# A new order of steps on five engines and in the load queue, in a fused linear-attention and dense-Mish kernel

## The chip, the cores and the metric

The kernel runs on one core of one Trainium2 chip. The metric is device time in microseconds of one launch. Three runs of the kernel before gave 151.34, 151.38 and 151.34 us; their median is 151.34. A profile of one execution lies beside them. Its span, from the first instruction to the last, is 148.7 us.

The core has five engines, each with a queue of its own that runs strictly in program order: TensorE (PE, with its weight loads as PEld), VectorE (DVE), ScalarE (ACT), GpSimd (POOL) and SyncE (SP), which here only issues DMAs. Engines wait for each other through semaphores.

## The reference

x has 2048 tokens of 448 columns. It is normalised per token, and two branches work on the result: a linear attention with 16 heads of 28 columns, whose feature map is softmax(p) beside softmax(-p), and a dense layer of 1792 columns with a Mish activation. The three are summed. Cut to what matters:

```python
xn = _layernorm(x)                                       # (1, 2048, 448)
q, k, v = heads of xn @ wqkv                             # 16 heads of 28
pq, pk = q @ w_phi, k @ w_phi                            # per head
phi_q = concat(softmax(pq), softmax(-pq))                # 56 features
phi_k = concat(softmax(pk), softmax(-pk))
kv, z = phi_k^T v, sum over tokens of phi_k
o = (phi_q kv) / (phi_q z + 1e-6)
h = xn @ w1 + b1                                         # 1792 columns
act = h * tanh(log(1 + exp(h)))                          # Mish
out = x + o @ wo + act @ w2
```

## The kernel before

**Tiles.** The tokens lie in 16 tiles t of 128; a pair of tiles is a unit u, 0 to 7. All of x stays in SBUF (x_all). The normalised x of a unit (xn, four buffers in turn) is transposed into xnT, seven blocks of 128 columns. w_phi is folded into the key and query weights at the head of the program: the key weights are transposed by TensorE (L556), multiplied by a block-diagonal Wbd (L580), and evacuated from PSUM into Wpk; the query weights come transposed by DMA and give Wpq.

**Order.** Nothing in the program decides at run time. The string ORDER lists 341 steps. `run_order` calls them one after another; each step appends its instructions to the queues of its engines and takes PSUM banks (four pairs of banks, the one used longest ago first). Waits follow from what each instruction reads and writes. So a step's place decides its place in the queue of every engine that it uses, and also which PSUM bank it waits for.

**Steps, by name** (a last letter a, d, p, m or s says the engine: ACT, DVE, POOL, DMA, SP; b says ACT and DVE):

- `lx..`, `lkm`, `lkt`, `lvm`, `lqT`, `lp`, `l1`, `l2`, `lo`: loads on SP (x; key, value and query weights; w_phi as Wraw; W1, W2, Wo). `lx0` to `lx3` carry one unit each, `lx4` and `lx6` two.
- `st`, `rs`, `xn`, `xt`: mean and variance of a unit (`st2b` and `st3b` leave one tile of the unit to ACT, L453 to L458), 1/std, normalisation (L497 on DVE, L492 on POOL), transposition (L505 on PE with an evacuation, or L517 by DMA).
- `z12`: twelve matmuls on zeros (L364) ahead of all others. `wtk`, `wmk`, `wmq`: the folding of the weights.
- `v`, `k`, `q` with parts A, B, H: value, key and query projections of a unit (L423). A and B are six matmuls of 64 rows each, H two, 448 columns wide. Two matmuls on different halves of the array run at the same time. After a unit's last part its result is evacuated: value to v_all (L510 on ACT or L512 on DVE), key and query as two exponentials on ACT (L618, L680).
- `kn`: normalisation of one sign of the keys of a unit: sum (L626) and reciprocal (L628) on DVE, product (L630) on POOL. Both signs of all eight units: 16 of them.
- `kv`: phi_k^T v of a unit, 32 small matmuls (L649), summed over all units in one bank. `ep`: the epsilon column (L353, L356, DVE). `kvz`: the sum goes to KVT (L660, DVE) and by DMA transposition to KVZ (L666).
- `e`: DMA transposition of a tile's query features to EqT (L688). `f`: one of 28 blocks of the dense layer (L423, 512 columns, parts A, B, H as above), with its Mish on ACT (L699). `nd`: numerator and denominator of a tile (L722) and seven DVE instructions. `ot`: DMA transposition of a unit's o (L757). `wo`, `g`: the output products (L845, L828). `sto`: stores.

The steps that the change touches at the head are these: `ln_stats` reads x and is the first thing that DVE and ACT do; `ln_pair` writes xn; `xT` transposes it; `w_tr` and `w_mm` fold the weights. The last of the folding's evacuations is what the first key matmul waits for.

Of the kernel before, what the change touches and what calls it, by code (L numbers as in the profile page):

```python
# [38 lines left out]
class Program:  # L39
# [46 lines left out]
    def dma(self, eng, fn, r=(), w=(), tag=""):  # L86
        return self.op(eng, fn, r, w, dma=True, tag=tag)
# [57 lines left out]


ORDER = """
pv table lx2s lba zero pm st2b lx3s lkms lps st3b lkts z12 pi b1 rs2p pw rs3a xn2d bd lx1s wtk0b lvms lx4s xn3d xt2b
wtk1b wmk0b lqT2 xt3a v2Ha wmk1a v2Ba lqT0 st1 v3Ha lqT1 lqT3 rs1a v3Aa v2Aa st4 rs4p pk v3Ba k3H lx0s k3A qd xn1d
wmq0d wmq1a k2H k3B lx6s pp k2A st5 q3A xn4d k2B q3B rs5p q2A xt1m l1ts q3H k1A q2H xn5p xt4m st0 v1Ad k1H st6 xt5m e7  # L150
rs0p q2B st7 xn0d v1Bd k1B v1Hd rs7p rs6p k4A k4H q1B k4B xn6d q1H q1A v4Ad k5H xn7d v4Hd k5A v4Bd v5Ad kn1.0 xt0m k5B
v5Bd k0B xt6m v5Hd xt7m v0Ba kn2.1 kn2.0 k0H k0A e3 k6H k6A kn0.0 e2 v6Ba l1ms k6B v0Ha kn0.1 v0Aa v6Aa v6Ha k7H k7A
q4B e6 k7B v7Aa v7Ha kn7.0 q4H q4A q6A q6H v7Ba e9 q6B kn6.0 f0.2B kn5.1 f0.0A f1.2A f0.2A f0.0H f1.2H kn6.1 e5 f1.3B
f0.2H f0.0B e12 f1.2B f1.3A kn4.1 f0.3B kn5.0 f1.3H e13 f0.3H f0.1B e4 f0.3A f0.1H f0.1A q7H q0A kn3.1 q0H kn4.0 q5B
e8 q0B q7B kv5 kn7.1 e0 kv0 kv2 q7A q5A f0.13A q5H f0.13B kv7 kv4 e10 kv6 f0.13H f0.6H f0.6A kn3.0 f0.10A f0.6B kn1.1
f0.10B kv3 kv1 ep f0.10H f1.7H f1.7A e11 f1.9A kvz f1.7B f0.12B f1.5B f0.12A f1.5H f0.5H f1.9H f0.12H l2s f1.9B f1.5A
f0.5A f1.1A nd3 f1.1B f0.5B e15 f1.0A f1.1H f1.13B f1.0H f1.13H f1.0B nd2 los f1.13A ot1m f1.8B f0.9H f1.8A f1.8H nd0
f0.11B f0.9A f0.11A f0.11H f0.7A f0.7H f0.8B nd6 e14 f0.8H f0.9B f0.7B e1 f0.8A f1.12H f1.12A f1.10A nd7 f1.10B f1.4H
f1.10H f1.12B ot3m f1.4A nd1 f1.6B f1.4B f0.4H f1.6A ot0m f0.4A wo1H f1.6H f0.4B nd4 wo1A wo3A wo1B wo3H nd5 ot2m g1
g3 g2 f1.11A f1.11H nd11 wo0B f1.11B wo3B wo0A nd13 wo0H nd10 g6 ot5m g0 g7 g11 nd12 wo2A wo5A sto1 ot6m wo5H wo2B  # L160
nd15 nd9 g10 sto0 g5 nd14 ot7m wo2H wo5B nd8 g4 g9 g14 g13 g12 g8 sto3 ot4m wo4H wo4A wo6B wo7B sto2 wo6H wo6A sto5
wo4B sto4 wo7H wob wo7A g15 stt14 sto6 stt15
"""


# [5 lines left out]
def _kernel(es, nc, A_x, A_wqkv, A_w_phi, A_wo, B_w1, B_b1, B_w2, out):  # L171
    def sb(name, shape, dtype):
        return es.enter_context(nc.sbuf_tensor(name, shape, dtype))
# [20 lines left out]
    xnT = sb("xnT", [P, NU, 7, P], BF16)  # L194
# [58 lines left out]
    def bank16(b):  # L253
        return PS.bitcast(BF16)[:, 2 * b * TCW:2 * (b + 1) * TCW]
# [7 lines left out]
    def pb(b):  # L262
        return ("ps", b)
# [238 lines left out]
    def transpose7(e, b, src, cut=7):  # L502
        for c in range(7):
            to = bank16(b)[:, c * P:(c + 1) * P] if c < cut else bank16(b + 1)[:, (c - cut) * P:(c - cut + 1) * P]
            ins = e.transpose(to, src[:, c * P:(c + 1) * P], ident[:])  # L505
        return ins

    def evac(eng, dst, src, r, w, tag):
        if eng == "ACT":
            op("ACT", lambda e: e.activation(dst(), src(), ACT.Copy), r=r, w=w, tag=tag)  # L510
        else:
            op("DVE", lambda e: e.tensor_copy(dst(), src()), r=r, w=w, tag=tag)  # L512

    def xT(u, eng):
        i = u % NXN
        if eng == "DMA":
            dma("SP", lambda e: e.dma_start_transpose(xnT[:, u, :, :], xn[i][:, :]),  # L517
                r=[("xn", i, 0, 0), ("xn", i, 1, 0), ("xn", i, 1, 1)], w=[("xnT", u), ("xnU", u)], tag=f"xTm{u}")
            return
        if eng == "both":  # L520
            b = take2(False)
            pe(lambda e: transpose7(e, b, xn[i], 3), [("xn", i, 0, 0), ("xn", i, 1, 0), ("xn", i, 1, 1), ("ident",)],
               [pb(b), pb(b + 1)], f"xT{u}")
            evac("ACT", lambda: xnT[:, u, 0:3, :].rearrange("p c n -> p (c n)"), lambda: bank16(b)[:, 0:3 * P], [pb(b)],
                 [("xnT", u)], f"xTe{u}")
# [453 lines left out]
```

## Time and profile before

| | us |
|---|---|
| median of three runs | 151.34 |
| span of the profiled execution | 148.7 |
| of it PE busy | 144.3 |
| DVE, ACT, POOL busy | 102.4, 74.5, 38.8 |
| end of PE's last matmuls of L828 at full width | 145.67 |

For the profiled execution no time but its span is given; the median of the runs lies 2.64 us above it.

How to read it: the page gives each engine's busy time and its share of the span, then the chain of work that ended last, by engine and line. A line of the code can carry several kinds of work: L423 serves the projections of v, k and q and the dense layer, told apart by the tiles' names (Wkv, Wpk, Wpq, W) and widths. A timeline row says when a group of instructions started, how long it lasted, engine, line, output and inputs, and in brackets for how long its engine had been idle and what ended that. A row of waits says which engine and line waited for which, the sum, how often, and the longest. The key tiles' exponentials lie in rows of actT, so L630 is written actT<-actT,rSk.

### The profile page before, as it was taken

The numbers are of one execution on the slowest core, as the hardware profiler recorded it, in microseconds if no ns is written. First come the engines' busy times: TensorE is split into PE (matmuls) and PEld (weight loads), VectorE is DVE, ScalarE is ACT, GpSimd is POOL, SyncE is SP. The second block draws the span as 40 slices with busy tenths as digits, with TensorE's granted clock in tenths as the row PEclk, the third lists the DMA queues.
The fourth block names the chain that finished last, engine by engine and source line by source line (L and its number), as shares of the span: only waits on it lengthen the run. The fifth ranks groups of instructions, "written<-read, shape, count | busy, mean of one in ns | idle before, by whom it ended". The sixth has DMA issues, their size and how long they took to land.

```text
span 148.7 us, 3867 instructions
## 1 busy us (share of the span) xinstructions
PE 144.3 (97%) x1669; PEld 74.4 (50%) x1669; DVE 102.4 (69%) x229; ACT 74.5 (50%) x91; POOL 38.8 (26%) x53
## 2 busy tenths in 40 slices
PE   6999999999999999999999999999999999999993
PEld 2375555555544554444544445545555555555562
DVE  0599898996999940407697879539983999930072
ACT  3987999879999999657757762002000000000000
POOL 4423475079999993000000000000000000000000
PEclk9999999999999999999999999999999999999999
DMA  4998678799499159399856053120013040542005
GB/s 133 240 270 232 138 143 158 128 169 334 102 194 191 30 49 132 69 223 283 225 120 121 0 66 62 27 39 0 7 21 102 20 108 0 123 100 85 4 0 185
DMA packets 39964, 17.23 MB, mean 116 GB/s; under 512 B 33932, under 2 KB 39180, under 8 KB 39948
## 3 DMA queue, kind: packets, MB, share of 16 engines
q1 hardware_dynamic: 39776, 16.89, 53.4%
q8 instruction: 13, 0.21, 0.6%
q10 hardware_dynamic: 172, 0.10, 0.2%
q14 instruction: 3, 0.02, 0.0%
HBM read 7.02 MB, written 1.84 MB: 60 GB/s over the span
## 4 chain that ended last, share of the span: by engine, by line
PE 96%; DVE 1%; POOL 0%; issue 0%; POOLq 0%
PE PS L423 50%; PE PS L828 29%; PE PS L845 7%; PE PS L364 4%; PE PS L722 3%; PE PS L649 2%; PE PS L580 1%; DVE xn L497 1%; PE PS L505 1%; DVE x_all L793 0%; POOL v_all L339 0%; PE PS L556 0%; DVE x_all L814 0%; DVE b1T L512 0%; PE PS L693 0%
## 5 line engine op out<-in xcount | busy, mean ns | idle before, releaser
L423 PE MATMUL PS<-xnT,W 64*128 64x512 bf16 x392 | 44.8, 377 | 0.0
L828 PE MATMUL PS<-W,actT 128*128 128x448 bf16 (+1 forms) x224 | 42.9, 351 | 0.0
L699 ACT ACTIVATE actT<-PS,b1T 128x1024 bf16<-128x1024 f32 x28 | 29.8, 1112 | 22.1 <-PE PS L423 22.1
L828 PEld LDWEIGHTS PS<-W,actT 128*128 128x128 bf16 x224 | 21.5, 98 | 19.8 <-issue 0.3
L423 PEld LDWEIGHTS PS<-xnT,W 64*128 64x128 bf16 x392 | 18.0, 94 | 21.9 <-PE PS L423 1.9
L630 POOL TENSOR_TENSOR actT<-actT,rSk 128x896 bf16<-128x896 bf16 x16 | 26.6, 1699 | 5.1 <-DVE rSk L628 5.1
L793 DVE TENSOR_TENSOR x_all<-PS,x_all 128x448 bf16<-128x448 f32 (+1 forms) x16 | 9.2, 614 | 15.1 <-PE PS L845 10.5
L626 DVE TENSOR_REDUCE Sk<-actT 128x32 f32<-128x896 bf16 x16 | 16.6, 1037 | 1.1 <-ACT actT L618 1.1
L618 ACT ACTIVATE actT<-PS 128x896 bf16<-128x896 f32 x16 | 13.7, 920 | 1.8 <-PE PS L423 1.7
L423 PE MATMUL PS<-Wpk,xnT 64*128 64x448 bf16 x112 | 13.2, 349 | 0.0
L423 PE MATMUL PS<-Wkv,xnT 64*128 64x448 bf16 x112 | 12.9, 349 | 0.0
L423 PE MATMUL PS<-Wpq,xnT 64*128 64x448 bf16 x112 | 12.6, 349 | 0.0
L738 DVE COPY Sq<-PS 128x16 f32<-128x16 f32 x32 | 4.0, 167 | 12.0 <-PE PS L722 12.0
L462 DVE BATCH_NORM_STATS2 stats<-x_all 128x6 f32<-128x448 bf16 x14 | 8.4, 601 | 3.5 <-DMA x_all<-in_A_x_dram 3.5
L746 DVE TENSOR_TENSOR v_all<-v_all 128x464 f32<-128x464 f32 x16 | 10.3, 642 | 0.6
L742 DVE TENSOR_TENSOR v_all<-PS,Sq 128x464 f32<-128x464 f32 x16 | 10.3, 641 | 0.5
L749 DVE TENSOR_TENSOR xn<-v_all,rden 128x448 bf16<-128x448 f32 x16 | 10.0, 626 | 0.6
L744 DVE TENSOR_TENSOR v_all<-PS,Sq 128x464 f32<-128x464 f32 x16 | 10.1, 630 | 0.0
L680 ACT ACTIVATE actT<-PS 128x896 bf16<-128x896 f32 x10 | 8.6, 930 | 0.1
L423 PEld LDWEIGHTS PS<-Wpq,xnT 64*128 64x128 bf16 x112 | 5.4, 94 | 5.0 <-ACT actT L680 0.2
L423 PEld LDWEIGHTS PS<-Wkv,xnT 64*128 64x128 bf16 x112 | 5.4, 94 | 5.0 <-ACT actT L618 0.2
L423 PEld LDWEIGHTS PS<-Wpk,xnT 64*128 64x128 bf16 x112 | 5.4, 94 | 5.1 <-issue 0.2
(83 smaller groups left out, 119.3 us busy)
## 6 DMA issues: line engine op xcount, KB each, us to landing
W<-in_B_w_dram SPq DMA_DIRECT2D x1, 1568.0 KB, 9.3
out_dram<-x_all SPq DMA_DIRECT2D x7, 224.0 KB, 2.2
W<-in_B_w_dram SPq DMA_DIRECT2D x1, 1344.0 KB, 6.5
x_all<-in_A_x_dram SPq DMA_DIRECT2D x4, 224.0 KB, 3.0
x_all<-in_A_x_dram SPq DMA_DIRECT2D x2, 448.0 KB, 4.7
Wkv<-in_A_wqkv_dram SPq DMA_DIRECT2D x2, 336.0 KB, 5.1
Wo<-in_A_wo_dram SPq DMA_DIRECT2D x2, 336.0 KB, 5.9
W<-in_B_w_dram SPq DMA_DIRECT2D x2, 224.0 KB, 3.6
```

The lines of the kernel that those rows point to most:

```text
L423: ins = e.matmul(o, lhs(c, k), rhs(c, k), start=first and n == at[par][0], stop=last and n == at[par][-1])
L618: op("ACT", lambda e, s=s: e.activation(E_of(u)[:, s, :, :], two(b, D), ACT.Exp, scale=1.0 if s == 0 else -1.0), r=[pb(b), pb(b + 1)], w=[ ...
L626: op("DVE", lambda e: e.tensor_reduce(Sk[u][:, s, :], Eh(), AX.X, ALU.add), r=[("E", u, s)], w=[("Sk", u, s)], tag=f"Sk{u}.{s}")
L630: op("POOL", lambda e: e.tensor_tensor(Eh(), Eh(), ap_on(rSk[u][:, s, 0:1], [[1, 2 * H], [0, DH]]), ALU.mult), r=[("E", u, s), ("rSk", u, ...
L699: op("ACT", lambda e: e.activation(actT[:, fc, q * 1024:(q + 1) * 1024], bank(b, 2), ACT.Mish, bias=b1T[:, fc:fc + 1]), r=[("b1T",), pb(b) ...
L742: op("DVE", lambda e: e.tensor_tensor(tv(t1[i]), num(0), sx(1), ALU.mult), r=[pb(b), pb(b + 1), ("Sq", i, 1)], w=[("t1", i)], tag=f"ta{t}")
L744: op("DVE", lambda e: e.tensor_tensor(tv(t2), num(1), sx(0), ALU.mult), r=[pb(b), pb(b + 1), ("Sq", i, 0)], w=[("t2",)], tag=f"tb{t}")
L746: op("DVE", lambda e: e.tensor_tensor(t1[i], t1[i], t2, ALU.add), r=[("t1", i), ("t2",)], w=[("t1", i)], tag=f"tc{t}")
L749: op("DVE", lambda e: e.tensor_tensor(o_sb[(t // 2) % 2][:, t % 2, :].rearrange("p (h d) -> p h d", d=DH), t1[i][:, :, 0:DH], ap_on(rden[i ...
L793: op("DVE", lambda e: e.tensor_tensor(x_all[:, t, 0:n], bank(b)[:, 0:n], x_all[:, t, 0:n], ALU.add), r=[pb(b), ("x", t)], w=[("out", t)], ...
L828: ins = e.matmul(bank(b)[:, 0:width(t)], actT[:, fc, tok(t)], W2[:, fc, 0:width(t)], start=first and fc == 0, stop=last and fc == FC - 1)
L845: ins = e.matmul(bank(b)[:, 0:w], oT_of(u)[lo:hi, cc * P:(cc + 1) * P], Wo[lo:hi, cc, 0:w], start=first and n == at[par][0], stop=last and ...
```

## The change

The table ORDER is replaced, and one label in `xT` changes, which names an instruction and has no effect on it. The steps are the same ones, but for the engine letter of some: the evacuations of `xt2`, `wtk0` and `wtk1` go from two engines to one, unit 1 is transposed by TensorE in place of unit 3, unit 3 is normalised by POOL in place of DVE, the 1/std of units 2 and 4 is made by ACT and that of unit 3 by POOL, the two `wmq` change their engines, and the evacuations of the value tiles are shared out anew (units 1, 2, 3, 4 on ACT and 0, 5, 6, 7 on DVE; before, 0, 2, 3, 6, 7 and 1, 4, 5). One line of the table, and the label:

```diff
-pv table lx2s lba zero pm st2b lx3s lkms lps st3b lkts z12 pi b1 rs2p pw rs3a xn2d bd lx1s wtk0b lvms lx4s xn3d xt2b
+lx2s lx1s zero lkms lps pi lx3s table lkts lba pm st2b rs2a st1 xn2d rs1a pw xn1d z12 st3b wtk0d lvms xt2a b1 lx4s
...
-                 [("xnT", u)], f"xTe{u}")
+                 [("xnT", u)], f"xTh{u}")
```

What stands in the queues now is seen best in rows of the two programs, engine by engine, in program order.

**ScalarE at the head.** Rows are line, operation, output and inputs, size. L453 to L458 are the statistics of one tile (the tile of unit 2 stands above these rows in both), L476 and L478 make 1/std of a unit, L510 are evacuations of PSUM. Before:

```order
L453 ACTIVATE junk,mv<-x_all 128x448
L456 ACTIVATE rmean<-mv 128x1
L458 ACTIVATE junk,mv<-x_all,rmean 128x448
L476 ACTIVATE lnv<-mv,eps_col 128x2
L478 ACTIVATE rstd<-lnv 128x2
L510 ACTIVATE Eq<-PS 112x512
L510 ACTIVATE xnT<-PS 128x384
L510 ACTIVATE Eq<-PS 112x512
L510 ACTIVATE Wpk<-PS 128x448
L510 ACTIVATE xnT<-PS 128x896
L510 ACTIVATE Wpk<-PS 128x896
L476 ACTIVATE lnv<-mv,eps_col 128x2
```

and now:

```order
L476 ACTIVATE lnv<-mv,eps_col 128x2
L478 ACTIVATE rstd<-lnv 128x2
L476 ACTIVATE lnv<-mv,eps_col 128x2
L478 ACTIVATE rstd<-lnv 128x2
L453 ACTIVATE junk,mv<-x_all 128x448
L456 ACTIVATE rmean<-mv 128x1
L458 ACTIVATE junk,mv<-x_all,rmean 128x448
L510 ACTIVATE xnT<-PS 128x896 x2
L510 ACTIVATE Wpk<-PS 128x448
L510 ACTIVATE Wpk<-PS 128x896
L476 ACTIVATE lnv<-mv,eps_col 128x2
```

The statistics of unit 3's tile have moved behind the 1/std of units 2 and 1, and the four evacuations behind them are now two whole units of xnT and the two of Wpk. In SP's queue the x of unit 3 moves at the same time from second place to fifth, behind x of units 2 and 1, the key weights and Wraw.

**VectorE at the end of the key normalisation.** The number in Sk and rSk is the unit. L512 are value tiles, L353 and L356 the epsilon column, L660 the first thing done with the sum of kv. Before:

```order
L626 TENSOR_REDUCE Sk3<-actT 128x32
L628 RECIPROCAL rSk3<-Sk3 128x32
L626 TENSOR_REDUCE Sk1<-actT 128x32
L628 RECIPROCAL rSk1<-Sk1 128x32
L353 TENSOR_REDUCE epsT<-ident 128x1 x2
L356 SCALAR_TENSOR_TENSOR epsT<-epsT 128x1
L660 TENSOR_SCALAR KVT<-PS,epsT 30x8x28 x4
```

and now:

```order
L512 CAST v_all<-PS 128x32x28 x2
L626 TENSOR_REDUCE Sk0<-actT 128x32
L628 RECIPROCAL rSk0<-Sk0 128x32
L353 TENSOR_REDUCE epsT<-ident 128x1 x2
L356 SCALAR_TENSOR_TENSOR epsT<-epsT 128x1
L626 TENSOR_REDUCE Sk6<-actT 128x32
L628 RECIPROCAL rSk6<-Sk6 128x32
L626 TENSOR_REDUCE Sk6<-actT 128x32
L628 RECIPROCAL rSk6<-Sk6 128x32
L626 TENSOR_REDUCE Sk7<-actT 128x32
L628 RECIPROCAL rSk7<-Sk7 128x32
L626 TENSOR_REDUCE Sk5<-actT 128x32
```

The epsilon column has moved ahead of the last four normalisations (units 6, 6, 7 and 5), and two value tiles (units 6 and 0) stand just ahead of it. POOL's products follow the same order: its last four are those of units 6, 6, 7 and 5.

**TensorE around kv.** L649 is kv, L722 is nd, L423 with W is the dense layer and with Wpq the query projection. Before:

```order
L423 MATMUL PS<-Wpq,xnT 128x448 x28
L649 MATMUL PS<-actT,v_all 30x56 x96
L423 MATMUL PS<-Wpq,xnT 128x448 x12
L423 MATMUL PS<-xnT,W 128x512 x6
L423 MATMUL PS<-Wpq,xnT 128x448 x2
L423 MATMUL PS<-xnT,W 128x512 x6
L649 MATMUL PS<-actT,v_all 30x56 x96
L423 MATMUL PS<-xnT,W 128x512 x28
L649 MATMUL PS<-actT,v_all 30x56 x64
L423 MATMUL PS<-xnT,W 128x512 x72
L722 MATMUL PS<-KVZ,EqT 128x60 x16
```

and now:

```order
L423 MATMUL PS<-Wpq,xnT 128x448 x6
L423 MATMUL PS<-xnT,W 128x512 x2
L649 MATMUL PS<-actT,v_all 30x56 x256
L423 MATMUL PS<-xnT,W 128x512 x46
L722 MATMUL PS<-KVZ,EqT 128x60 x16
```

The three groups of kv have become one of 256 matmuls, in the order of units 3, 6, 4, 2, 7, 0, 5, 1, and 46 matmuls of the dense layer, in place of 72, stand between it and the first use of KVZ.

Three more moves matter for queues. On DVE the normalisation of units 6 and 7 (six instructions of L497) now comes after the first sum and reciprocal of a key unit (unit 2), whose product is the first of its kind on POOL; before, all of L497 came ahead of all of L626. On SP the main part of W1 now stands ahead of the transpositions of units 0, 6 and 7 (L517); before, behind them. And where nd had been mixed with g through the last third of the program, all dense blocks and thirteen of the sixteen nd now come ahead of the first g, so that g runs in three stretches of four, four and eight tiles.

More of the change, by code (lines that the diff above doesn't have):

```diff
@@ L147 @@
 ORDER = """
-pv table lx2s lba zero pm st2b lx3s lkms lps st3b lkts z12 pi b1 rs2p pw rs3a xn2d bd lx1s wtk0b lvms lx4s xn3d xt2b
[L149 to L162, printed above, removed]
+lx2s lx1s zero lkms lps pi lx3s table lkts lba pm st2b rs2a st1 xn2d rs1a pw xn1d z12 st3b wtk0d lvms xt2a b1 lx4s
@@ new lines @@
+bd xt1a lx0s rs3p wtk1d wmk0b wmk1a v2Ha xn3p lqT3 lqT0 st4 v1Ad rs4a lqT2 lqT1 v1Bd st5 k2H v2Ba xn4d lx6s v1Ha pp
+v2Aa xt3m qd k2A rs5p k2B xn5p st0 xt4m k1H wmq1d wmq0a k1A k1B st6 k3H l1ts xt5m st7 rs0p xn0d l1ms k3A xt0m q1H
+rs6p k3B k4H rs7p k4A k4B v4Hd kn2.1 q1B xn6d q1A q3H xn7d v4Ba v4Aa kn4.1 v5Ha q3B q3A v5Ad q2H v5Bd k5H kn2.0 q2A
+kn1.0 xt6m kn1.1 pv q2B k5A xt7m k5B v3Bd k7H k7B v3Ha k7A kn4.0 v7Ha v3Aa q4H v7Bd e7 v7Ad k0A e3 k0B kn3.0 k0H q6H
+q4A e2 e6 q4B e4 e5 kn7.1 q6B k6B v0Aa k6H q6A kn5.1 v0Ha kn0.1 v6Ba v6Aa k6A kn3.1 v6Hd e9 q5A v0Bd kn0.0 ep q5H
@@ new lines @@
+q5B e8 q7H kn6.1 q7B f1.3H q7A f1.3B kn6.0 f1.3A f0.0A f0.0H f1.1H f1.1B f1.1A f0.0B los f1.0H e14 f1.0A e13 f1.0B
+q0B kn7.0 q0H f1.2H e12 f1.2B q0A kn5.0 f0.8H kv3 pk e10 kv6 kv4 kv2 kv7 kv0 e15 kv5 kv1 f0.8B e1 f0.8A f0.2H kvz
+f0.2A e11 e0 f1.2A f0.2B f1.6H wob f0.5B f0.5A nd2 f1.6B f0.5H nd3 f1.6A f1.5H f1.5B f1.5A f0.10H f0.10A f0.10B
+f0.7H nd1 ot1m f0.11H f0.7A f0.7B f0.13H f0.13B f0.13A f0.3B nd6 f0.3H f0.11B f0.11A f0.6A nd7 f0.3A f0.6H f1.11H
+f0.6B f1.11B nd0 f0.4H f1.11A ot3m f0.4B ot0m f0.9H f0.9A f0.4A f0.12H nd4 f0.12B f0.12A f0.9B f1.7A nd10 l2s f1.13H
@@ L163 @@
+f1.13B f1.7B f1.7H f1.10H f1.10B f1.13A f1.10A f1.9B nd5 f1.9H f0.1H f0.1A f1.9A ot2m nd13 f1.4H f1.4B f0.1B f1.4A
+f1.8H f1.8A wo1A nd12 wo1H f1.12B f1.12A f1.12H f1.8B wo1B wo0A wo0B nd11 ot6m ot5m wo0H nd15 g0 g1 g3 g2 nd9 wo6A
+wo6H wo2H nd8 wo2B wo6B wo2A nd14 ot4m ot7m sto0 g12 g4 g13 g5 wo4H wo7B wo5H wo4A sto1 wo3H wo5B wo7H wo3B wo7A
+wo4B wo5A wo3A g10 g11 g14 stt14 g6 sto5 g9 g7 sto3 g8 sto2 sto6 g15 sto4 stt15
 """
```

## The prediction

> **What bounds the kernel now.** First the page: busy times (part 1) and the chain that ended last (part 4).
>
> ```profile
> PE 144.3 (97%) x1669; PEld 74.4 (50%) x1669; DVE 102.4 (69%) x229; ACT 74.5 (50%) x91; POOL 38.8 (26%) x53
> ...
> PE 96%; DVE 1%; POOL 0%; issue 0%; POOLq 0%
> ```
>
> TensorE is busy for 144.3 of 148.7 us and the chain lies on it for 96%. A busy share can hide waits, so next the waits of TensorE, and the chain in order of time (start, duration, what).
>
> ```profile
> PE PS L364 <- POOL mask L327: 1.4, 1, 1.4
> PE PS L505 <- DVE xn L497: 0.3, 1, 0.3
> PE PS L556 <- DMA Wkv<-in_A_wqkv_dram: 0.2, 1, 0.2
> ```
>
> ```profile
> 1.39 5.30 PE PS L364 x12
> ...
> 10.72 3.32 PE PS L423 x34
> ...
> 51.18 0.88 PE PS L649 x96
> ...
> 54.84 0.88 PE PS L649 x96
> ...
> 58.84 0.61 PE PS L649 x64
> 59.45 7.90 PE PS L423 x72
> ...
> 90.76 0.22 PE PS L722 x16
> ...
> 113.91 0.33 PE PS L722 x16
> ...
> 143.25 2.42 PE PS L828 x14
> 145.67 0.02 issue
> 145.69 0.56 DVE x_all L793
> ```
>
> All waits of TensorE end before 9 us. From 10.72 it runs at one pace to 145.67: 34 matmuls of 448 columns in 3.32 are 0.098 us each, 72 of 512 columns in 7.90 are 0.110. So a new order can win only at the head, at the switches between matmul shapes, and behind 145.67, where the last bank's addition and store stay as they were. It can lose wherever TensorE is made to wait. The matmuls are the same, so I add up delays of TensorE against this trace.
>
> **A. The head: +0.65 us.** Unit u is a pair of token tiles. The new load queue sends x of pair 1 second and x of pair 3 fifth. ScalarE still makes half of pair 3's statistics (L453 to L458), and these now stand in its queue ahead of both evacuations of the transposed x (xnT) and of both of Wpk; the first key matmul needs the last of them. Timeline of the head, and two rows of the DMA issues (KB each, us to landing):
>
> ```profile
> 2.20 0.49 SPq L293 DMA_DIRECT2D Wraw<-in_A_w_phi_dram  x1
> ...
> 2.72 1.20 SPq L278 DMA_DIRECT2D Wkv<-in_A_wqkv_dram  x2
> ...
> 3.54 0.58 ACT L453 ACTIVATE junk<-x_all 128x448 bf16<-128x448 bf16 x1 [1.46 <-DMA x_all<-in_A_x_dram]
> ...
> 5.14 0.56 ACT L453 ACTIVATE junk<-x_all 128x448 bf16<-128x448 bf16 x1
> ...
> 9.67 0.54 ACT L510 ACTIVATE Wpk<-PS 128x448 bf16<-128x448 f32 x1
> ...
> 9.86 0.36 PE L423 MATMUL PS<-Wkv,xnT 64*128 64x448 bf16 x2
> 10.09 0.92 ACT L510 ACTIVATE xnT<-PS 128x896 bf16<-128x896 bf16 x1
> ...
> 10.65 2.63 PE L423 MATMUL PS<-Wkv,xnT 64*128 64x448 bf16 x26
> ...
> 10.89 0.93 ACT L510 ACTIVATE Wpk<-PS 128x896 bf16<-128x896 f32 x1
> ```
>
> ```profile
> Wkv<-in_A_wqkv_dram SPq DMA_DIRECT2D x2, 112.0 KB, 5.0
> ...
> Wraw<-in_A_w_phi_dram SPq DMA_DIRECT2D x1, 24.5 KB, 5.0
> ```
>
> When does x of pair 3 land? It now stands right behind Wraw, which lands at 2.20 + 5.0 = 7.2. The 224 KB that stood there, two halves issued from 2.72 to 3.92, landed by about 8.4. The same bytes for x, so 7.2 to 8.4; I take 7.85, the middle. Then ScalarE needs 1.60 for the statistics (3.54 to 5.14), 0.80 for each xnT (10.09 to 10.89), 0.42 for the small Wpk (9.67 to 10.09) and 0.93 for the large one: 4.55, and about 0.05 to wake TensorE. Key matmuls start at 12.45. Ahead of them stand 14 value matmuls; before, two went at 9.86 and the next twelve from 10.65, so the 14th was done at 10.65 + 12 x 0.098 = 11.8. The delay is 12.45 - 11.8 = 0.65. Bounds: 0 (7.2) to 1.2 (8.4). The first warm-up starts some 0.4 earlier, but the matmul behind it still waits for Wkv, so that buys nothing.
>
> **B. Two waits inside the projections: +0.85 us together.** DVE and POOL rows of the key normalisation, DVE first:
>
> ```profile
> 49.08 1.03 DVE L626 TENSOR_REDUCE Sk<-actT 128x32 f32<-128x896 bf16 x1
> 50.14 0.35 DVE L628 RECIPROCAL rSk<-Sk 128x32 f32<-128x32 f32 x1
> 50.41 1.03 DVE L626 TENSOR_REDUCE Sk<-actT 128x32 f32<-128x896 bf16 x1
> ...
> 51.94 1.64 DVE L356 SCALAR_TENSOR_TENSOR epsT<-epsT 128x1 f32<-128x1 f32 x1
> ```
>
> ```profile
> 46.90 9.98 POOL L630 TENSOR_TENSOR actT<-actT,rSk 128x896 bf16<-128x896 bf16 x6
> ```
>
> ```profile
> 50.22 3.35 POOL L630 TENSOR_TENSOR actT<-actT,rSk 128x896 bf16<-128x896 bf16 x2
> ...
> L512 DVE CAST v_all<-PS 128x896 bf16<-128x896 f32 x2 | 2.2, 1090 | 0.1
> ```
>
> One half of a pair's normalisation costs DVE 1.33 (49.08 to 50.41) and POOL 1.66 (9.98 / 6). Before, the eight kv steps (L649) stood in three groups spread from 51 to 59 us, so POOL's multiplications ended beside them. Now all eight stand in one run, and the seventh, kv5, needs POOL's last product. Worse, the epsilon steps (L353, L356) have moved from the end of DVE's normalisations to a place ahead of the last four. The one-column L356 took 1.64 us: it started at 51.94 and ended at 53.58, and POOL's multiplication ended at 50.22 + 3.35 = 53.57. It waited for POOL. In the new order it starts just after rSk of pair 0, which also releases a POOL multiplication, so it will wait a whole one, and DVE's next normalisation, for which POOL waits, is late by that.
>
> The chain from the last value pass of pair 0: 0.2 to wake DVE, 1.0 for its evacuation (1.09 less overlap), 1.39 for the sum and reciprocal, 1.70 behind POOL, 1.41 for the next sum and reciprocal, 4 x 1.66 on POOL: 12.35 us. TensorE's own work between the same two points: 36 matmuls at 0.098, 66 at 0.110, six kv steps of 0.27 (0.88 - 0.61) and a switch: 12.5. No slack is left, and DVE reaches that evacuation with a full queue: from its evacuation of pair 5 it has 3 x 1.0 + 9 x 1.33 = 15.0 us, plus a wait of about 0.4 for pair 7, against 158 matmuls, 14.9 to 15.5 us. I expect kv5 to wait 0.3 to 0.6.
>
> The other place is the key matmul of pair 7, which waits for the DMA transposition of its x. That is issued when DVE has normalised pair 7, and these six instructions (L497) now stand beside POOL's first multiplication.
>
> ```profile
> L497 DVE TENSOR_SCALAR xn<-x_all,mv,rstd x6: 286/374/622, 6.9 to 8.8; 128x448 bf16<-128x448 bf16 x2, 128x64 bf16<-128x64 bf16 x2, 128x384 bf16<-128x384 bf16 x2
> ```
>
> ```profile
> W<-in_B_w_dram SPq DMA_DIRECT2D x1, 1344.0 KB, 6.5
> ...
> xnT<-xn SPq DMA_TRANSPOSE x6, 3.1
> ```
>
> The 622 ns one lay beside a POOL product, so at least 0.25 was lost there (622 - 374). Carried along the new order with the durations above, the transposition lands within 0.1 us of its use if POOL lets DVE by, and up to 0.9 late if DVE waits a whole POOL instruction (1.66, less the slack). The 1344 KB of W1 now also go ahead of the last three transpositions. Both waits overlap, since a wait at pair 7 gives POOL time: together 0.3 to 1.8, and I take 0.85, nearer to the rows (0.25 and 0.3 to 0.6 measured or worked out) than to the worst.
>
> [...]
>
> **C. The wait for KVZ: +0.25.** From the end of kv to the landing of its transposition:
>
> ```profile
> 59.59 1.83 DVE L660 TENSOR_SCALAR KVT<-PS,epsT 30x224 bf16<-30x224 f32 x4 [6.01 <-PE PS L649]
> ```
>
> ```profile
> 61.46 1.23 SPq L666 DMA_TRANSPOSE KVZ<-KVT  x1
> ...
> DMA to landing us min/median/max: 3.2/3.2/3.2
> ```
>
> That is 64.66 - 59.45 = 5.2 us. Before, 72 matmuls (7.9 us) covered it; now 46 stand between, 5.05 us, so with the wake-up a wait of 0.1 to 0.4.
>
> **D. Fewer switches: -0.75.** Where matmuls of 128 rows meet those of 64, or of 56 (L722), the step is longer: 0.33 against 0.22. Such meetings fall from nine to five: -0.45. The kv steps in one run take 0.61 + 6 x 0.27 = 2.23, not 2.37, and two entries into them go, at 0.11 each: -0.35 in all. I take -0.75; 0 to -0.9.
>
> **Sum.** 0.65 + 0.85 + 0.25 - 0.75 = +1.0 us. Of the profiled execution only the span is told: 148.7 becomes 149.7. The median lies 2.64 above the span (151.34 - 148.7), which I add unchanged: **152.3 us**. Behind kv I find no other wait: the weights W2 are issued far ahead of the first L828, and each bank taken for L722 is free again one or two units later.
>
> **Rivals.** *No blocking (0.15):* L356 gets in between two POOL instructions. The chain to kv5 is 1.5 shorter, B is zero, and A + C + D = +0.15: 151.5. Against it: the place of L356 right behind what releases POOL. *Faster (0.15):* TensorE's own path decides everywhere. Its place is the load of pair 3's x: landing at 7.2, just behind Wraw, makes A zero; with B at zero too, only C and D are left, -0.5: 150.85. It decides once x lands before about 7.5 and L356 isn't blocked. For it speaks that nothing else in the new order costs TensorE time. *Much slower (0.15):* DVE waits for POOL at pair 7 in full and x lands at 8.4: A 1.2, B 1.6, C 0.3, D -0.75, so +2.35: 153.7. [...] The forecast keeps 0.55.
>
> **The numbers.** The forecast's own range is 151.8 to 153.0. Eight in ten needs most of the no-blocking case and of the much slower one: 151.0 to 153.6. Within 0.2% (0.3 us), about what a measurement of this kernel can tell from no change, lies the no-blocking case: 0.15. Faster takes 0.15, slower 0.70.
>
> **What would show it.** Right: in the new profile L356 again takes over 1 us; TensorE waits at L649 for POOL actT, at L423 for DMA xnT, at L722 for the DMA of KVZ, and near 11 us for ACT. The first key matmul near 12.4 shows A. Wrong: no wait of TensorE after 13 us (then B is zero), a short L356, or x of pair 3 landing near 7.2.

## The result, and the profile after

The changed kernel takes **167.73 us** (median of 4 runs, 167.08 to 168.31) against 151.36 (151.34 to 151.42) for the kernel before: a ratio of 1.108, with a 95% interval of 1.104 to 1.112. Forecast were 152.3 us and a range of 151.0 to 153.6. The direction was right, the size was off by 15 us. The span of the profiled execution is 165.2 us; the median lies 2.5 above it, much as before (2.64).

From the page of the kernel after: the busy times, the clock granted to TensorE in 40 slices of 4.13 us, and the chain that ended last.

```profile
PE 152.5 (92%) x1669; PEld 72.3 (44%) x1669; DVE 104.9 (64%) x227; ACT 74.5 (45%) x90; POOL 39.8 (24%) x54
...
PEclk9999999999999995699999999999999999999999
...
PE 76%; DVE 11%; issue 4%; DMA 4%; SPq 2%; POOL 1%; DVEq 0%
```

The same 1669 matmuls keep TensorE "busy" for 8.2 us longer, the chain lies on it for 76% in place of 96%, and two slices show about half a clock. None of that was in the forecast. Next the waits of TensorE (engine and line, what it waited for, us in total, times, longest), matmuls first and then its weight loads:

```profile
PE PS L649 <- issue: 4.1, 2, 2.2
...
PE PS L423 <- DVE rSk L628: 0.4, 1, 0.4
```

```profile
PEld PS L423 <- PE PS L423: 21.7, 44, 1.0
```

and the same row of weight loads in the kernel before:

```profile
PEld PS L423 <- PE PS L423: 1.9, 6, 0.3
```

The us of this row are idle time of the weight loads, not delay of TensorE (21.7 of idle time against 9.0 of delay in the table below), which works off other matmuls meanwhile; what such a wait costs is read from the starts of matmuls below.

**TensorE waits for itself.** Weight loads of L423 that waited for a matmul of L423 were 6, and are 44. The reason stands in the printed code: `pe_pass` makes a pass wait for the last pass of the other side on the same banks, since `passes` gives A and H one assignment of array halves and B the opposite one. In the old order another unit's pass always stands between two such passes. In the new one 39 stand directly behind each other: `q5H q5B`, `f1.3B f1.3A` and so on. Of the 44 waits 38 are such places (the 39th, `wo0A wo0B`, is a wait of L845); at the other six, as at the six before, another pass lies between, and TensorE loses next to nothing: 0.220 to 0.226 us from one pair of matmuls to the next, at full pace 0.186 (448 columns) and 0.212 (512). Timeline of the kernel after (start, duration, what), where q2A q2B and then k5A k5B follow each other:

```profile
27.34 1.54 PE L423 MATMUL PS<-Wpq,xnT 64*128 64x448 bf16 x12
28.71 1.54 PE L423 MATMUL PS<-Wpk,xnT 64*128 64x448 bf16 x12
30.09 0.73 PE L423 MATMUL PS<-Wkv,xnT 64*128 64x448 bf16 x6
```

and the same passes in E3 (below), taken in turn:

```profile
27.37 0.73 PE L423 MATMUL PS<-Wpq,xnT 64*128 64x448 bf16 x6
27.94 0.73 PE L423 MATMUL PS<-Wpk,xnT 64*128 64x448 bf16 x6
28.51 0.73 PE L423 MATMUL PS<-Wpq,xnT 64*128 64x448 bf16 x6
29.07 0.73 PE L423 MATMUL PS<-Wkv,xnT 64*128 64x448 bf16 x6
```

From start to start, twelve matmuls take 1.37 us in the first and 2 x 0.57 = 1.14 in the second: 0.23 for each such place.

**The kv run stops twice.** Timeline of TensorE after, around kv (L649); the bracket is the idle time before a row and what ended it:

```profile
57.13 1.17 PE L649 MATMUL PS<-actT,v_all 128*30 128x56 bf16 x123
60.16 1.21 PE L649 MATMUL PS<-actT,v_all 128*30 128x56 bf16 x128 [1.85 <-issue]
63.62 0.27 PE L649 MATMUL PS<-actT,v_all 128*30 128x56 bf16 x5 [2.24 <-issue]
63.82 8.01 PE L423 MATMUL PS<-xnT,W 64*128 64x512 bf16 x46
```

"issue" means that no engine released it. The middle row holds exactly 128 matmuls; with their 128 weight loads these are 256 instructions. The page counts 13 packets in an "instruction" queue, and 13 x 256 = 3328 fits TensorE's 2 x 1669 = 3338 instructions. In the DMA view around kv one of these packets falls in each of the windows 57.5 to 58, 61 to 62 and 64 to 65 (starts at 57.77, 61.31 and 64.77) and none between; the rows of the first two (packets, MB, share of the 16 engines):

```profile
q8 instruction: 1, 0.02, 11.6%
...
q8 instruction: 1, 0.02, 6.3%
```

So the run used up a block in 1.2 us, a new one came only every 3.5 us, and TensorE went on 2.3 to 2.4 us after a packet's start (60.16 and 63.62). Each of the 13 packets has 16384 bytes in the trace (0.21 MB in all); how many blocks stand ready, no run here shows. The places agree too: in every trace with such pauses (after, E2, E4, E6 and E8 to E12) they stand behind TensorE's 600th matmul or its 726th to 728th, in whatever step that falls, so I take it that a block ends there.

**Then the clock falls.** Windows of the kernel after (us, length and busy PE, granted clock, DMA share, GB/s):

```profile
57.00:62.00 5.00, 2.52 (x253) 1.00 0.38 74
62.00:69.00 7.00, 5.32 (x29) 0.51 0.30 59
69.00:72.00 3.00, 2.93 (x42) 1.00 0.70 130
```

The clock records of the trace say it more closely: half clock from 62.09 to 68.92. In all traces that show a change, the stretches from one change to the next are whole multiples of 3.41 us: here 17 at full clock (58.03), then 2 at half (6.83); in E2, E9 and E12 the half clock lasts only one.

To add this up, each of TensorE's 231 steps was found in the trace, and from the time between its start and the next start its matmuls at full pace were taken off. What is left is delay, us:

| | before | after | E1 | E3 | E10 |
|---|---|---|---|---|---|
| head, up to the first projection | 4.2 | 4.9 | 5.0 | 5.1 | 4.9 |
| waits for the opposite pass directly ahead | 0 | 9.0 | 9.5 | 0.5 | 0.2 |
| kv, entries included | 0.9 | 5.2 | 0.9 | 1.3 | 2.7 |
| dense passes at half clock | 0 | 2.7 | 0 | 0 | 0 |
| all else (shape switches, waits for engines) | 3.6 | 3.7 | 5.4 | 11.7 | 8.2 |
| sum | 8.7 | 25.5 | 20.8 | 18.6 | 16.1 |

The new order costs 16.8 us of delay (its first matmul starts 0.4 earlier; the spans differ by 16.5), and the three rows in the middle hold 16.0 of it. The forecast knew none of the three as a cost.

### The profile page after: what moved, and what is told of

Its sections match the earlier page's. It is cut to its first block, busy times and chain, and to the rows that moved or that the text cites. A ratio compares the mean times of both kernels' runs of the same rounds, so it can differ in the third digit from the quotient of the medians.

```text
span 165.2 us, 3859 instructions
## 1 busy us (share of the span) xinstructions
PE 152.5 (92%) x1669; PEld 72.3 (44%) x1669; DVE 104.9 (64%) x227; ACT 74.5 (45%) x90; POOL 39.8 (24%) x54
## 4 chain that ended last, share of the span: by engine, by line
PE 76%; DVE 11%; issue 4%; DMA 4%; SPq 2%; POOL 1%; DVEq 0%
PE PS L423 40%; PE PS L828 26%; PE PS L845 7%; DMA x_all<-in_A_x_dram 4%; DVE stats L462 3%; DVE Sk L626 2%; DVE xn L497 2%; PE PS L722 2%; PE PS L649 2%; DVE mv L464 1%; SPq L270 1%; SPq L278 1%; DVE rSk L628 1%; DVE Wpq L512 1%; DVE v_all L512 1%
## 5 line engine op out<-in xcount | busy, mean ns | idle before, releaser
L423 PE MATMUL PS<-xnT,W 64*128 64x512 bf16 x392 | 50.9, 392 | 1.3
L699 ACT ACTIVATE actT<-PS,b1T 128x1024 bf16<-128x1024 f32 x28 | 30.4, 1112 | 24.4 <-PE PS L423 24.3
L828 PEld LDWEIGHTS PS<-W,actT 128*128 128x128 bf16 x224 | 21.7, 98 | 20.1 <-issue 0.4
L423 PEld LDWEIGHTS PS<-xnT,W 64*128 64x128 bf16 x392 | 17.1, 97 | 28.6 <-PE PS L423 11.3
L630 POOL TENSOR_TENSOR actT<-actT,rSk 128x896 bf16<-128x896 bf16 x16 | 26.8, 1699 | 7.9 <-DVE rSk L628 6.9
L793 DVE TENSOR_TENSOR x_all<-PS,x_all 128x448 bf16<-128x448 f32 (+1 forms) x16 | 9.7, 618 | 26.8 <-PE PS L828 26.8
L626 DVE TENSOR_REDUCE Sk<-actT 128x32 f32<-128x896 bf16 x16 | 16.7, 1046 | 0.0
L423 PE MATMUL PS<-Wpk,xnT 64*128 64x448 bf16 x112 | 14.0, 351 | 0.9 <-DVE rSk L628 0.4
L423 PE MATMUL PS<-Wpq,xnT 64*128 64x448 bf16 x112 | 14.0, 351 | 0.5
L423 PE MATMUL PS<-Wkv,xnT 64*128 64x448 bf16 x112 | 13.6, 350 | 0.3
L423 PEld LDWEIGHTS PS<-Wpk,xnT 64*128 64x128 bf16 x112 | 4.7, 94 | 8.4 <-PE PS L423 4.0
L423 PEld LDWEIGHTS PS<-Wpq,xnT 64*128 64x128 bf16 x112 | 4.9, 94 | 7.5 <-PE PS L423 3.8
L660 DVE TENSOR_SCALAR KVT<-PS,epsT 30x224 bf16<-30x224 f32 x4 | 1.8, 448 | 9.5 <-PE PS L649 9.5
```

What stands on the lines that cost most here:

```text
L423: ins = e.matmul(o, lhs(c, k), rhs(c, k), start=first and n == at[par][0], stop=last and n == at[par][-1])
L626: op("DVE", lambda e: e.tensor_reduce(Sk[u][:, s, :], Eh(), AX.X, ALU.add), r=[("E", u, s)], w=[("Sk", u, s)], tag=f"Sk{u}.{s}")
L630: op("POOL", lambda e: e.tensor_tensor(Eh(), Eh(), ap_on(rSk[u][:, s, 0:1], [[1, 2 * H], [0, DH]]), ALU.mult), r=[("E", u, s), ("rSk", u, ...
L699: op("ACT", lambda e: e.activation(actT[:, fc, q * 1024:(q + 1) * 1024], bank(b, 2), ACT.Mish, bias=b1T[:, fc:fc + 1]), r=[("b1T",), pb(b) ...
L828: ins = e.matmul(bank(b)[:, 0:width(t)], actT[:, fc, tok(t)], W2[:, fc, 0:width(t)], start=first and fc == 0, stop=last and fc == FC - 1)
```

## Experiments

**Theory 1:** a pass directly behind the opposite pass of its bank costs about 0.235 us. **Theory 2:** the kv run outpaces the fetch of instructions, and its pauses pull the clock down. **Rivals:** these places only fill time in which other engines are late anyway, or the pauses wait for something else of the new order.

| | change | us (median of 4) | ratio to before (95%) |
|---|---|---|---|
| E1 | after, kv in three groups | 162.09 | 1.072 (1.068 to 1.075) |
| E2 | after, 16 places behind kv apart | 165.50 | 1.095 (1.091 to 1.099) |
| E9 | after, 13 places gone by names | 163.70 | 1.081 (1.075 to 1.087) |
| E3 | E1 with 37 places apart | 160.13 | 1.059 (1.056 to 1.063) |
| E5 | before, 10 places made | 154.10 | 1.019 (1.016 to 1.022) |
| E4 | before, kv in one run | 156.56 | 1.033 (1.028 to 1.039) |
| E12 | the same without E4's wait | 155.44 | 1.026 (1.020 to 1.031) |
| E6 | after, kv in two groups | 163.19 | 1.077 (1.073 to 1.081) |
| E7 | E3, two DVE steps put back | 159.45 | 1.055 (1.049 to 1.061) |
| E8 | E7, queries of unit 0 early | 159.42 | 1.054 (1.048 to 1.060) |
| E11 | E8, W1 later on SP | 158.77 | 1.049 (1.046 to 1.052) |
| E10 | all remedies | 158.06 | 1.044 (1.042 to 1.046) |

**E1, kv in three groups.**

```diff
-kn6.1 q7B f1.3H q7A f1.3B kn6.0 f1.3A f0.0A f0.0H f1.1H f1.1B f1.1A f0.0B los f1.0H e14 f1.0A e13 f1.0B
-q0B kn7.0 q0H f1.2H e12 f1.2B q0A kn5.0 f0.8H kv3 pk e10 kv6 kv4 kv2 kv7 kv0 e15 kv5 kv1 f0.8B
+kn6.1 q7B f1.3H q7A f1.3B kn6.0 f1.3A f0.0A f0.0H kv2 kv1 kv4 f1.1H f1.1B f1.1A f0.0B los kv3 kv0 f1.0H e14 f1.0A e13
+f1.0B q0B kn7.0 q0H f1.2H e12 f1.2B q0A kn5.0 f0.8H kv6 kv7 kv5 pk e10 e15 f0.8B
```

> The changed kernel with its eight kv steps in three groups again (2, 1, 4 / 3, 0 / 6, 7, 5), each a few dense passes apart; the 39 places where a pass of TensorE follows directly on the opposite half of its own bank stay. Theory 2 (the run of 256 small matmuls outpaces the fetch of TensorE's instructions, and the pauses drop its clock): the two pauses of 1.85 and 2.24 us and the half clock of about 2.5 us go, two more entries into kv cost 0.2; 167.7 - 6.4 = 161.3 (160.5 to 162.0), the granted clock near 1.00. Theory 1 alone (only the passes that wait for TensorE itself count, and the pauses in kv are a wait for something else that comes again): 167 to 168.

162.09 us, 5.6 less, just above the range given. Its timeline of L649:

```profile
50.88 0.95 PE L649 MATMUL PS<-actT,v_all 128*30 128x56 bf16 x96
...
54.50 0.69 PE L649 MATMUL PS<-actT,v_all 128*30 128x56 bf16 x64
...
60.17 0.95 PE L649 MATMUL PS<-actT,v_all 128*30 128x56 bf16 x96
```

Both pauses are gone and the clock is 1.000 throughout. Theory 1 alone is out. In the profiled execution, the slowest of the four (162.41), what is missing to 6.4 is longer waits, chiefly this one for a transposed x:

```profile
PE PS L423 <- DMA xnT<-xn: 1.3, 2, 0.7
```

They stand at 18 and 31 us, ahead of the first step that E1 moves, where the two programs are the same. So they are not of E1's making: they differ from one execution to the next.

**E2, 16 places behind kv taken apart** by exchanging passes with neighbours, as in

```diff
-f1.6A f1.5H f1.5B f1.5A f0.10H f0.10A f0.10B
+f1.5H f1.6A f1.5B f0.10H f0.10A f1.5A f0.10B
```

> The changed kernel with kv still in one run; behind kv 16 of the 39 adjacent opposite passes of one bank are taken apart by exchanging passes with a neighbour or two. Theory 1 (each such place costs TensorE about 0.235 us): 16 x 0.235 = 3.8 less, 163.9 (163.3 to 164.7). Rival (the end is set by VectorE and ScalarE there, TensorE's waits for itself only fill gaps): under 1 less, 167.

165.50, 2.2 less: between the two. The step account tells why: dense and output passes lost 3.7 us of delay, but the steps nd gained 1.5, since a pass that opens a bank earlier or closes it later (f1.5H, f0.12A) now waits for VectorE or ScalarE. That 3.7 comes near 16 x 0.235 = 3.8 is in part luck: it also holds about 0.8 less loss at half clock (one stretch of 3.41 us in place of two) and about as much in new waits between dense passes. So it was not a clean test. E9 is a cleaner one.

**E9, names alone.** A and B are equal work, so exchanging the two letters in a unit moves no step, yet H then stands beside the pass of its own half. Thirteen units, such as

```diff
-q5A v0Bd kn0.0 ep q5H q5B
+q5B v0Bd kn0.0 ep q5H q5A
```

> The changed kernel with the letters A and B exchanged in 13 units (k7, k0, q5, q7, q0 and eight dense blocks), so that H stands beside the pass of its own half; A and B are equal work, and no step changes its place on any engine. Adjacent opposite passes: 26 in place of 39. Theory 1: 13 x 0.235 = 3.05 less, 164.7 (164.2 to 165.3); five of them lie ahead of kv, where a later wait may take some of it back, up to 1.2, so at most 165.9. Rival (the adjacency is not the cause): 167.2 to 168.2.

163.70 (162.8 to 164.6 by the interval): 4.0 less, where 3.05 was expected. Weight loads that waited for a pass fell from 44 to 31, by the 13:

```profile
PEld PS L423 <- PE PS L423: 15.5, 31, 1.0
```

The remaining us lies mostly in the half-clock stretch, one of 3.41 us in this profile and two in that of after (mean clock 0.989 and 0.979). Executions with the same mean clock differ by 2.9 (at 0.979: 164.82 against 167.74, the median of three) and by 3.7 (one of after, at 0.990: 167.08; the median of three of E9, at 0.989: 163.42), on either side of theory 1's 3.05. Theory 1 holds: by its edit nothing but the waits of TensorE for itself was touched.

**E5, the price in the kernel before.** Ten places made behind kv, as in

```diff
-f0.12B f1.5B f0.12A f1.5H
+f0.12B f0.12A f1.5B f1.5H
```

> The kernel before, with 10 adjacent opposite passes of one bank made behind kv by exchanging neighbouring passes; nothing else. Theory 1: 10 x 0.235 = +2.35, 153.7 (153.3 to 154.1). Rival (such a wait costs only where the order is already late): 151.4 to 151.8.

154.10, 2.7 more (2.4 to 3.4 by the interval). The ten steps hold 2.39 us of delay, 0.24 each; the rest are 0.8 of waits of nd. The row of weight loads goes from 6 to 10; eight of these are new places (the other two are waits of L845), two are left of the old six:

```profile
PEld PS L423 <- PE PS L423: 5.1, 10, 0.6
```

So the price holds in an order that is tight otherwise, and the rival (a cost only where the order is late) is out.

**E4 and E12, the kv run in the kernel before.**

```diff
-e8 q0B q7B kv5 kn7.1 e0 kv0 kv2 q7A q5A f0.13A q5H f0.13B kv7 kv4 e10 kv6 f0.13H f0.6H f0.6A kn3.0 f0.10A f0.6B kn1.1
-f0.10B kv3 kv1 ep f0.10H
+e8 q0B q7B kn7.1 e0 q5A q7A f0.13A q5H f0.13B e10 f0.6H f0.13H f0.6A kn3.0 f0.10A f0.6B kn1.1 f0.10B kv5 kv0 kv2 kv7
+kv4 kv6 kv3 kv1 ep f0.10H
```

> The kernel before with its three kv groups drawn together into one run of 256 matmuls at the place of the last group (two passes exchanged so that no opposite passes of one bank become neighbours); nothing of the new order. Theory 2: two pauses of about 2 us in the run (4.2), then a half clock for some 6 us (2.5 lost), 0.35 saved at entries: 151.4 + 6.4 = 157.8 (155.5 to 158.5), granted clock 0.98. Rival (the pauses need something else of the new order, the transpositions of Eq beside them or POOL): 151.0 to 151.8, clock 1.00.

156.56, 5.1 more. The mean clock was 0.978 in the profiled execution and one other (157.1 and 157.2 us) and 1.000 in the other two (156.0 both): there 4.5 is left without a lower clock. But one of its two pauses was a wait for a Mish. The key features lie in rows 6 to 13 of actT, which the dense blocks overwrite, and here blocks 0.6 and 0.13 close ahead of kv: kv0 and kv7 use overwritten rows, and kv0 waited 2.37 us for ScalarE. E12 removes that by exchanging blocks 0.6 and 1.1, and 0.13 and 1.0, wherever they stand:

```diff
-q5A q7A f0.13A q5H f0.13B e10 f0.6H f0.13H f0.6A kn3.0 f0.10A f0.6B kn1.1 f0.10B kv5
+q5A q7A f1.0A q5H f1.0B e10 f1.1H f1.0H f1.1A kn3.0 f0.10A f1.1B kn1.1 f0.10B kv5
```

> The kernel before with all eight kv in one run of 256 matmuls at the place of the last group, as in E4, but with dense blocks 0 and 1 of the second half of the tokens (1.0 and 1.1) in the places of blocks 0.13 and 0.6, so that no kv step has to wait for a Mish or reads a row that a dense block has overwritten. Theory 2: one or two pauses in the run that no engine ends, 1.9 to 4.5 in all, and a stretch at half clock behind them, 1 to 2.5: 154.3 to 158. Rival (only the wait for ScalarE of E4 cost time; the one pause there came from the fetch being late behind it): 151.0 to 152.3.

155.44, 4.1 more, with one pause that no engine ends, and then the clock (timeline, then windows, as above):

```profile
57.17 2.04 PE L649 MATMUL PS<-actT,v_all 128*30 128x56 bf16 x191
61.90 0.97 PE L649 MATMUL PS<-actT,v_all 128*30 128x56 bf16 x65 [2.69 <-issue]
```

```profile
55.00:63.00 8.00, 5.32 (x280) 0.90 0.70 86
63.00:70.00 7.00, 7.00 (x58) 0.87 0.59 133
```

kv's delay rises by 3.3 and that of the dense passes by 0.9. Theory 2 holds without anything of the new order. Here 191 matmuls went ahead of the pause, in the kernel after 123: the run begins elsewhere in TensorE's stream, and the pause stands behind the 726th matmul, in the kernel after behind the 728th.

**E6, groups of four.**

```diff
-f0.0B los f1.0H
+f0.0B los kv2 kv1 kv4 kv3 f1.0H
...
-f0.8H kv3 pk e10 kv6 kv4 kv2 kv7 kv0 e15 kv5 kv1 f0.8B
+f0.8H kv0 kv6 kv7 kv5 pk e10 e15 f0.8B
```

> The changed kernel with its 39 adjacent places, kv in two groups of four (128 matmuls and 128 weight loads each, 256 instructions, one 16 KB block of them) some 4 us apart. Against three groups (162.1): if a reserve of at least one block stands ready ahead of a run, no pause, 161.9 to 162.4; if the reserve is what was left in the block begun, one pause of 0.5 to 2.3 in one or both groups, 162.6 to 166, and no half clock unless both pauses fall together.

163.19. One group (TensorE's matmuls 440 to 567) ran through; the other (606 to 733), in which the 728th lies, paused there, by less than in one run, and the clock stayed at 1.000:

```profile
52.98 1.44 PE L649 MATMUL PS<-actT,v_all 128*30 128x56 bf16 x128
...
59.09 1.17 PE L649 MATMUL PS<-actT,v_all 128*30 128x56 bf16 x123
61.63 0.23 PE L649 MATMUL PS<-actT,v_all 128*30 128x56 bf16 x5 [1.37 <-issue]
```

**E3, both causes removed** (E1's groups and 37 exchanges like E2's).

> The changed kernel with kv in three groups and 37 of the 39 adjacent places taken apart. Theories 1 and 2 together: 167.7 - 6.4 - 37 x 0.235 = 152.6; with TensorE 5 us earlier at kv, the waits forecast for POOL's last products come back, up to +1: 152.2 to 153.6. Rival (a third cause of several us, the head or a wait on VectorE): above 155.

160.13: a miss of 7.5 us, and the rival's case. The table shows where it went: 9.0 us of waits for itself went away, 6.3 came back as other waits. The largest rows among TensorE's waits in E3:

```profile
PE PS L423 <- ACT Eq L680: 1.4, 1, 1.4
PE PS L423 <- DMA xnT<-xn: 1.3, 1, 1.3
```

The first stands behind kv, for the second exponential of unit 0's queries; the second is the key matmul of pair 7, the very place of part B. With TensorE slowed by itself, most of these had been covered. Some are of the experiment's own making: 1.5 us stand at nd, as in E2.

**E7, E8, E11, the places that E3 uncovered.** E7 puts the normalisation of units 6 and 7 ahead of the first key sum on DVE and the epsilon column behind the last; E8 also moves unit 0's queries ahead of the dense blocks; E11 also moves the load of W1.

```diff
-k4A v4Hd k4B kn2.1 q1B xn6d q3H xn7d v4Ba
+k4A v4Hd k4B q1B xn6d q3H xn7d kn2.1 v4Ba
...
-q5A v0Bd kn0.0 ep q5H
+q5A v0Bd kn0.0 q5H
...
-q0A kn5.0 f0.8H kv6
+q0A kn5.0 ep f0.8H kv6
```

E8 against E7, and E11 against E8:

```diff
-q5B e8 q7H kn6.1 f1.3H q7A f1.3B q7B kn6.0 f1.3A f0.0A kv2 kv1
+q5B e8 e13 e12 q7H kn6.1 q0H q7A q0A q7B kn6.0 q0B f1.3H f0.0A f1.3B f0.0H f1.3A kv2 kv1
...
-xn0d l1ms k3A xt0m
+xn0d k3A xt0m
...
-q2B xt7m v3Bd
+q2B xt7m l1ms v3Bd
```

> E3 (kv in three groups, 37 places taken apart, 160.1) with two steps of VectorE put back as in the kernel before: the normalisation of units 6 and 7 ahead of the first key sum, and the epsilon column behind the last key normalisation. Theory (part B of the forecast: VectorE held up by POOL there makes the key matmul of pair 7 wait, 1.47 in E3, and kv wait): 1.2 to 1.9 less, 158.2 to 158.9. Rival (the waits in E3 come from banks that ScalarE frees late, so a wait taken away comes back at the next bank): 159.6 to 160.4.

> The kernel of E7 with the three passes of unit 0's queries and the two transpositions that free their buffer moved ahead of the first dense block, so that ScalarE loads the table for Mish once and not, with a detour to the exponential, three times. Theory (in E3 TensorE waits 1.62 behind kv for the second exponential of unit 0): 1.4 to 2.4 below E7, since the detour is two table loads of 1.28. Rival (ScalarE has idle time there, so the detour is hidden): within 0.4 of E7.

> E8 with the load of the main part of W1 (1344 KB) issued behind the transposition of pair 7, as in the kernel before, no longer ahead of those of pairs 0, 6 and 7. Theory (in E7's profile SyncE was held 3.03 us at the transposition of pair 6 behind that load, and the key matmul of pair 7 waited 1.55): those waits and the one at the key matmul of unit 0 (0.86) go in every execution, 0.8 to 2.0 below E8 (159.4): 157.4 to 158.6. Rival (the transposed x is late for another reason, or ScalarE's exponentials set that place): within 0.4 of E8.

159.45 (runs from 159.0 to 161.0), 159.42 and 158.77: the interval of each overlaps that of the one before, so no single step is shown by its time; all three together are (1.059 in E3, 1.049 in E11, intervals apart). Each gave less than its theory said. Their traces show the waits changing places. In E7 VectorE has x of pair 7 ready at 23.9, not at 26.2 as in E3, but the key matmul still waits 1.4: the issue of the three transpositions of units 0, 6 and 7, behind the load of W1, takes SyncE 5.70 us and ends at 28.03, as in E3 (27.99). In E8, with nothing changed there, it takes 4.64, and that matmul does not wait. The row of E7:

```profile
22.33 5.70 SPq L517 DMA_TRANSPOSE xnT<-xn  x3
```

In E8 the wait for unit 0's exponential is gone, but kv pauses for 1.0 us in two places again: its second group (matmuls 550 to 613) now spans the 600th, and the third, in which the 727th lies, follows it after 2.65 us of dense passes, in E7 after 4.0.

**E10, all remedies.** E11's edits with 38 places gone, 13 of them by names.

> All remedies in one: kv in three groups, 38 of the 39 adjacent places gone (13 by letters, the others by exchanges chosen not to close a unit late), the DVE order of E7, unit 0's queries early, W1 behind the transposition of pair 7. If the waits found so far are all, what remains against the kernel before is the head (about 1) and small waits for banks: 153.5 to 156. If the new order is tight at many more places: 156.5 to 159.

158.06, in the upper case. No version beat the kernel before. What remains, by TensorE's waits:

```profile
PE PS L649 <- issue: 1.4, 2, 0.8
PE PS L423 <- DMA xnT<-xn: 1.2, 1, 1.2
...
PE PS L423 <- ACT actT L618: 0.8, 1, 0.8
```

The last column of the table holds it: against before 0.7 more in the head, 1.8 in kv (the groups of three and two pause here, with 2.65 and 2.2 us of other passes ahead of them) and 4.6 at many places, each a transposed x or a bank that ScalarE or VectorE frees late.

## Why the prediction was wrong

**The step that failed** stands at the end of the first part: "All waits of TensorE end before 9 us", and from it that TensorE "can lose wherever TensorE is made to wait" by another engine. It was read from the rows of its matmuls alone. The row of its weight loads, with 1.9 us of waits for L423 itself, and the wait that `pe_pass` builds in were left out. Fed with the new order, that rule gives 39 places. At the 0.23 to 0.25 that the after trace shows this is 9 us; E9 and E5 confirm it. The forecast put it at nothing: "Behind kv I find no other wait", and "nothing else in the new order costs TensorE time". The price was not in the trace of before, where no two such passes touch, but the 39 could have been counted.

**D, fewer switches (-0.75), had the wrong sign.** "The kv steps in one run" was booked as a saving of 0.35. The run cost 4.3 us of pauses and 2.7 at half clock, and E1 gave 5.6 back. The switches themselves did get fewer: the steps nd and g hold 1.1 us of delay beyond full pace, before 1.5, close to the -0.45 of the forecast.

That the direction was right is luck: of the 16.8 us of delay the forecast's own terms hold about 1 (0.7 in the head, 0.4 at pair 7), and D booked a saving where the run cost 7.0.

**A, the head (+0.65), had ScalarE's work right and TensorE's wait wrong.** ScalarE at the head of the kernel after, then TensorE:

```profile
7.27 0.58 ACT L453 ACTIVATE junk<-x_all 128x448 bf16<-128x448 bf16 x1 [0.85 <-DMA x_all<-in_A_x_dram]
...
8.88 1.70 ACT L510 ACTIVATE xnT<-PS 128x896 bf16<-128x896 bf16 x2
10.47 1.35 ACT L510 ACTIVATE Wpk<-PS 128x448 bf16<-128x448 f32 x2
```

```profile
10.62 1.74 PE L423 MATMUL PS<-Wkv,xnT 64*128 64x448 bf16 x14
12.20 0.35 PE L423 MATMUL PS<-Wpk,xnT 64*128 64x448 bf16 x2
```

From 7.27 to 11.82 are the 4.55 us of the sum; x of pair 3 landed at the low end (7.2), not at 7.85. Key matmuls began at 12.20 against 11.8 before, but not because of ScalarE, which was done 0.4 earlier: the 14 value matmuls filled TensorE from 10.62 on, with one place of 0.24 (`v1Ad v1Bd`) in them. The row shows no idle time, and no wait for ScalarE stands among TensorE's. The 0.7 that the head did cost lies ahead of that, in waits for the key weights and for xn (1.0 and 0.7 us, before 0.2 and 0.3), less the earlier start.

**B, two waits in the projections (+0.85), had VectorE's blocks right and TensorE's waits mostly wrong.** L356 and the worst L497 took a whole POOL instruction: 1680 ns, to 49.05 us, beside a product of 1700 to 49.04, and 1685, to 24.96, beside one of 1699 to 24.92. One row each:

```profile
L356 DVE SCALAR_TENSOR_TENSOR epsT<-epsT x1: 1680/1680/1680, 47.4 to 47.4; 128x1 f32<-128x1 f32 x1
```

```profile
L497 DVE TENSOR_SCALAR xn<-x_all,mv,rstd x18: 286/370/1685, 5.8 to 25.7; 128x448 bf16<-128x448 bf16 x6, 128x64 bf16<-128x64 bf16 x6, 128x384 bf16<-128x384 bf16 x6
```

The second row has 1685 ns against a median of 370. The forecast did not put this into its sum in full. But TensorE lost only 0.4 at pair 7 and nothing at kv5. It did not wait for POOL at kv5 in E3 either, where it was less late itself. At pair 7 it waited 1.3 in E3, but in E7, where no L497 took over 0.40, it waited as long: there SyncE's queue behind the load of W1 held the transposition, so the block of L497 alone does not set this wait.

**C, the wait for KVZ (+0.25),** did not come: half-clocked passes covered it. In E1, at full clock, it was 0.2.

**The rivals** all varied the same four terms, so none could hold the time. The clock that was lost in the middle (0.51 from 62 to 69 us) is in none of the four.

## What to carry to other kernels

When an order changes, count the waits of an engine for itself too, in the rows of its weight loads and in the code's own extra dependences: they cost little each here (0.24 us), but there were 39 of them. A dense run of small matmuls is not free because it is on one engine: here it used up 256 instructions in 1.2 us, got 256 every 3.5, and stood still for 4.1. So compare the two, and look where in the run the pauses fall. And a removed wait pays only up to the next one: of 9.0 us taken away in E3, 6.3 came back elsewhere.

## What was not expected of the hardware

- In the kernel after, a pass that waited for the opposite half on its own banks started 0.23 to 0.25 us late, whether it was two or six matmuls long; in E5 0.24.
- The packets of the instruction queue, 13 for TensorE's 3338 instructions, fit blocks of 256, and runs of small matmuls paused in two places, behind the 600th matmul and behind the 726th to 728th. Runs of 128 matmuls and more paused there for 1.4 to 2.7 us at a time, though E12 only at the second such place in its run. The groups of 64 and 96 paused for 0.28 to 0.81 in E8, E10 and E11, with 2.2 to 2.65 us of other passes ahead of each, and crossed the 727th without a pause in E1, E3 and E7, with 4.0 to 5.0 us ahead. The three groups of the kernel before (482 to 577, 604 to 699, 728 to 791) and the first of E6 cross none of these places.
- The clock fell to half after pauses of 1.85 and 2.24 us with 1.2 us of work between, and after a single one of 2.69 (E12); after one of 1.37 (E6) it stayed. In every trace with a change it changed on a grid of 3.41 us. The five falls around kv (after, E2, E4, E9, E12) came at the end of a grid window in which TensorE had stood idle for 2.2 to 2.6 us in all; windows with 1.3 to 1.7 idle (E2, E3, E6, E7, E9) brought none. So where the grid lay against the pauses may decide, which fits that executions of one kernel had different mean clocks (E4: 0.978 and 1.000). No window here was idle throughout: in the kernel after, 2.2 idle of 3.41 were enough.
